# One row of w4 by loads of 125 and 3 partitions of its own

## The chip, the core and the metric

The kernel runs on one core of a Trainium2 chip. The metric is the device time of one execution, in microseconds (us). The core has five engines with instruction streams of their own: PE (matrix products, with weight loads shown as PEld), DVE (vector work), ACT (activation functions), POOL and SP. Data come from the chip's main memory by 16 DMA engines. SP issues almost all loads here; a load is cut into packets that the 16 DMA engines carry, and each DMA engine works through its packets of SP's queue in the order of issue.

## What is computed

The reference decodes one token (x has shape 1 x 1 x 1024). It normalises x, sends it through an attention block over a cache of 65,536 keys and through a small MLP block, and adds x and both results:

```python
def reference(A_x, A_k_cache, A_v_cache, A_wq, A_wo, B_x, B_w1, B_w2, B_w3, B_w4):
    ...
    xn = _layernorm(x, axis=-1)
    return x + _A_ref(xn, A_k_cache, A_v_cache, A_wq, A_wo) + _B_ref(xn, B_w1, B_w2, B_w3, B_w4)
```

`_A_ref` makes 32 query heads of 128 with wq, scores them against 4 groups of cached keys, takes the softmax, sums the cached values and multiplies by wo. `_B_ref` is two gelu layers with w1 and w2, then `gelu(layernorm(x1) @ w3) @ w4`, with 1024 inputs, 3584 hidden values and 1024 outputs, so w4 is 3584 x 1024. With one token, the shifted rows between w1 and w2 are all zero, and nearly all the time is reading: 170 MB of caches and weights, in bf16.

## The kernel before

Every large operand passes through one of three slots (`big`, `SLOTS = 3`) of 128 partitions by 64 KB. The list `items` gives the order of loading and of work: wq, K(0,0), V(0,0), w3, w12 (w1 and w2 in one slot), then K and V of the four groups and two halves of the keys, with w4 put in just ahead of the last V, and at the end wo in three slots (pieces of 20, 8, and 3 + 1 rows of 1024, `WO_PIECES`). So the end of the list is K(3,1), w4, V(3,1), wo 0, wo 1, wo 2.

`ensure` keeps the loads two items ahead of the work (`LOOKAHEAD = 2`): before item i is worked on, item i + 2 is issued. `issue` (L96 and below) takes a slot, builds the list `loads` of source and place, and issues each on SP (L118 and L119). SP waits there until the slot's former content has been used, and the next load waits behind it in SP's stream. A K load is 128 packets of 64 KB, 8 on each DMA engine; w4 was one load (L104): partition m takes the rows 28m to 28m + 27 of w4, 28 rows of 1024 bf16 values, 57,344 bytes.

The work on an item: `compute_K` transposes the keys on DVE (L337), multiplies them by the queries on PE (L340), finds the maximum (L344), and makes the exponentials (L357) and their transposes (L359). `compute_V` multiplies these by the values (L393). `compute_w4` makes 28 x 4 small products (`row_acc`, L161), each with one row of 1024 of a partition, which add to psB; `compute_wo` does the same with wo, and after its last piece copies psB (L435) and stores the result (L436). Two small loads of x are issued by ACT at the start; the one at L130 brings x as 4 rows of 512 bytes to the partitions 0, 32, 64 and 96.

Of the kernel before, what the change touches and what calls it, by code (L numbers as in the profile page):

```python
# [22 lines left out]
def kernel(  # L23
# [14 lines left out]
    nc = tc.nc  # L38
    P = 128
# [9 lines left out]
    FC = F // P  # L49
    NOUT = A_wo.shape[1]  # L50
# [23 lines left out]
    wq_v = A_wq.rearrange("(p c) n -> p (c n)", c=DC)  # L74
    w3_v = B_w3.rearrange("(p c) f -> p (c f)", c=DC)
    w4_v = B_w4.rearrange("(m c) n -> m (c n)", c=FC)
    wo_v = A_wo.rearrange("(m c) n -> m c n", c=OC)
    w1_v = B_w1.rearrange("(p c) n -> p (c n)", c=DC)
    w2_v = B_w2.rearrange("(m c) n -> m (c n)", c=DC)
# [16 lines left out]
    def issue(item):  # L96
        kind = item[0]
        t = big.tile([P, KEYS], BF16, name="slot")
        if kind == "wq":
            loads = [(0, wq_v)]  # L100
        elif kind == "w3":
            loads = [(0, w3_v)]
        elif kind == "w4":
            loads = [(0, w4_v)]  # L104
        elif kind == "w12":
            loads = [(0, w1_v), (KEYS // 2, w2_v)]
        elif kind == "wo":
            pieces = [item[1]] if item[1] < 2 else list(range(2, len(WO_PIECES)))
            loads = []
            for q in pieces:  # L110
                c0 = wo_start[q]
                at = (c0 - wo_start[pieces[0]]) * NOUT
                loads.append((at, wo_v[:, c0:c0 + WO_PIECES[q], :].rearrange("p c n -> p (c n)")))
        else:
            cache = A_k_cache if kind == "K" else A_v_cache
            _, g, r = item
            loads = [(0, cache[0, g, r * KEYS:(r + 1) * KEYS, :].rearrange("(p k) d -> p (k d)", p=P))]
        for at, src in loads:  # L118
            nc.sync.dma_start(out=t[:, at:at + src.shape[-1]], in_=src)  # L119
        st[item] = t  # L120

    x_bf = const.tile([P, DC], BF16, name="x_bf")
# [11 lines left out]
    def ensure(upto):  # L134
        while n_issued[0] <= min(upto, len(items) - 1):
            issue(items[n_issued[0]])
            n_issued[0] += 1
# [30 lines left out]
    def layernorm(src, tag):  # L168
# [50 lines left out]
                          in_=sel8[:].unsqueeze(2).to_broadcast([P, 8, 4]))  # L219

    iv = ident_bf[:].rearrange("p (b i r) -> p b r i", b=2, r=2)
    for b in range(2):
        for par in range(2):
            nc.vector.tensor_copy(out=psel[:, 2 * b + par, :].rearrange("p (a i) -> p a i", a=4),
                                  in_=iv[:, b, par, :].unsqueeze(1).to_broadcast([P, 4, 32]))
# [4 lines left out]
                          in_=lead.unsqueeze(2).to_broadcast([P, 4, 16]))  # L230
    gsel = const.tile([P, P], BF16, name="gsel")
    nc.vector.tensor_copy(out=gsel[:].rearrange("p (j m) -> p j m", j=2),
                          in_=lead[:, 0:2].unsqueeze(2).to_broadcast([P, 2, 64]))
# [239 lines left out]
```

## Time and profile before

Three runs took 402.79, 402.89 and 403.63 us. The profile is of another execution:

| what | value |
|---|---|
| median of three runs | 402.89 us |
| the profiled execution's own time | 402.66 us |
| its span, from the first instruction to the last | 400.9 us |
| granted PE clock, mean | 0.796 |
| busy: PE, DVE, ACT, POOL | 204.0, 209.0, 27.3, 5.9 us |
| read by DMA | 169.87 MB, 424 GB/s over the span |
| w4's load: issue, and landing of its last share | 323.72, 358.62 us |
| w4's products on PE (L161 with hT) | from 363.01 us on |

The span divided into 40 slices shows the same picture from the first to the last but one (the DMA row is the mean busy share of the 16 DMA engines in tenths, below it GB/s):

```profile
DMA  9999999999999999999999999999999999999994
GB/s 406 425 425 419 419 420 452 401 489 419 425 433 419 419 484 427 419 432 438 420 419 471 432 420 438 438 420 438 451 419 425 433 445 436 419 455 419 414 416 174
```

PE and DVE are each busy for about half of the span and idle in between; the DMA engines are not. The loads that matter for the change are these (KB of one, and the time from issue to landing in us; the first line is w3 and w4 together, the last is the fourth piece of wo, 2,048 bytes for each of 128 partitions):

```profile
slot<-in_B_w_dram SPq DMA_DIRECT2D x2, 7168.0 KB, 37.7
...
slot<-in_A_wo_dram SPq DMA_DIRECT2D x1, 5120.0 KB, 27.0
...
slot<-in_A_wo_dram SPq DMA_DIRECT2D x1, 2048.0 KB, 26.3
slot<-in_A_wo_dram SPq DMA_DIRECT2D x1, 768.0 KB, 13.5
slot<-in_A_wo_dram SPq DMA_DIRECT2D x1, 256.0 KB
```

### The profile page before, as it was taken

The numbers are of one execution on the slowest core, as the hardware profiler recorded it, in microseconds if no ns is written. First come the engines' busy times: TensorE is split into PE (matmuls) and PEld (weight loads), VectorE is DVE, ScalarE is ACT, GpSimd is POOL, SyncE is SP. The second block draws the span as 40 slices with busy tenths as digits, with TensorE's granted clock in tenths as the row PEclk, the third lists the DMA queues.
The fourth block names the chain that finished last, engine by engine and source line by source line (L and its number), as shares of the span: only waits on it lengthen the run. The fifth ranks groups of instructions, "written<-read, shape, count | busy, mean of one in ns | idle before, by whom it ended". The sixth has DMA issues, their size and how long they took to land.

```text
span 400.9 us, 3366 instructions
## 1 busy us (share of the span) xinstructions
PE 204.0 (51%) x1489; PEld 85.4 (21%) x1489; DVE 209.0 (52%) x190; ACT 27.3 (7%) x33; POOL 5.9 (1%) x27
## 2 busy tenths in 40 slices
PE   0016393660079148741965295529453935496235
PEld 0003131220023013310322042204121412143113
DVE  0022992230196559634954894279358841885120
ACT  0002002110000300020002000100200020002000
POOL 1010000000000000000000000000000000000000
PEclk9999698695569587967895689679975976599588
DMA  9999999999999999999999999999999999999994
GB/s 406 425 425 419 419 420 452 401 489 419 425 433 419 419 484 427 419 432 438 420 419 471 432 420 438 438 420 438 451 419 425 433 445 436 419 455 419 414 416 174
DMA packets 3773, 170.07 MB, mean 424 GB/s; under 512 B 552, under 2 KB 560, under 8 KB 816
## 3 DMA queue, kind: packets, MB, share of 16 engines
q1 hardware_dynamic: 3608, 169.87, 98.1%
q8 instruction: 11, 0.18, 0.2%
q10 hardware_dynamic: 152, 0.00, 0.0%
q14 instruction: 2, 0.02, 0.0%
HBM read 169.87 MB, written 0.00 MB: 424 GB/s over the span
## 4 chain that ended last, share of the span: by engine, by line
DMA 48%; PE 26%; DVE 20%; ACT 4%; issue 1%; ACTq 0%; SPq 0%; POOL 0%; DVEq 0%
DMA slot<-in_A_k_cache_dram 28%; PE sc L340 14%; DVE slot L337 12%; DMA slot<-in_A_v_cache_dram 10%; PE oacc L393 8%; DMA work<-in_A_x_dram 7%; DMA slot<-in_A_wo_dram 3%; DVE work L359 3%; DVE mx L344 3%; ACT work L357 3%; PE rows L242 1%; ACT L357 1%; PE pm_mx L346 0%; DVE m L348 0%; DVE og L408 0%
## 5 line engine op out<-in xcount | busy, mean ns | idle before, releaser
L340 PE MATMUL sc<-slot,qst 128*128 128x512 bf16 x512 | 129.8, 415 | 75.6 <-DVE slot L337 75.6
L337 DVE STREAM_TRANSPOSE slot<-slot 128x4096 f32<-128x4096 f32 x32 | 139.4, 4413 | 49.4 <-DMA slot<-in_A_k_cache_dram 49.3
L340 PEld LDWEIGHTS <-qst 128*128 128x128 bf16 x512 | 52.1, 103 | 152.1 <-DVE slot L337 55.9
L393 PE MATMUL oacc<-slot,work 128*32 128x512 bf16 x512 | 43.3, 513 | 45.3 <-DVE work L359 35.7
L344 DVE TENSOR_REDUCE mx<-sc 128x1 f32<-128x2048 f32 x8 | 18.3, 2292 | 30.2 <-PE sc L340 30.2
L393 PEld LDWEIGHTS <-work 128*32 128x32 bf16 x512 | 16.3, 124 | 69.2 <-DVE work L359 36.3
L357 ACT ACTIVATE work<-sc,nball 128x2048 bf16<-128x2048 f32 x8 | 15.7, 1967 | 193.5 <-DVE nball L355 193.5
L359 DVE STREAM_TRANSPOSE work<-work 128x2048 bf16<-128x2048 bf16 x8 | 18.5, 2311 | 19.1 <-ACT work L357 19.1
L408 DVE SCALAR_TENSOR_TENSOR og<-oacc,wm,og 128x128 f32<-128x128 f32 x16 | 5.6, 351 | 22.2 <-PE oacc L393 21.8
L172 PE MATMUL pm_ln<-ln_rowsum_a,work 128*128 128x1 f32 x2 | 0.6, 362 | 27.7 <-POOL work L147 27.7
L166 DVE CAST xT<-x_bf 128x8 f32<-128x8 bf16 x1 | 0.2, 172 | 22.0 <-DMA x_bf<-in_A_x_dram 22.0
L346 PE MATMUL pm_mx<-ident_f,mx 128*1 128x128 f32 x8 | 2.3, 283 | 18.1 <-DVE mx L344 18.1
L242 PE MATMUL rows<-slot,xpad 128*32 128x512 bf16 (+1 forms) x144 | 9.6, 397 | 0.9 <-DMA slot<-in_B_w_dram 0.9
L161 PE MATMUL psB<-slot,oT 128*1 128x256 bf16 x128 | 6.3, 362 | 6.3 <-DMA slot<-in_A_wo_dram 6.1
L357 ACT ACT_TABLE_LOAD x2 | 2.6, 1283 | 73.5 <-DVE nball L355 73.5
L287 DVE TENSOR_TENSOR work<-pm_h,mask 128x448 f32<-128x448 f32 x1 | 0.6, 625 | 11.4 <-PE pm_h L284 11.4
L172 PEld LDWEIGHTS pm_ln<-ln_rowsum_a,work 128*128 128x128 f32 x2 | 0.5, 310 | 27.6 <-POOL work L147 27.6
L435 DVE CAST work<-psB 97x256 bf16<-97x256 f32 x1 | 0.4, 425 | 11.4 <-PE psB L161 11.4
L161 PEld LDWEIGHTS <-oT 128*1 128x1 bf16 x128 | 3.9, 108 | 8.8 <-issue 5.6
L242 PEld LDWEIGHTS <-xpad 128*32 128x32 bf16 x144 | 4.4, 103 | 5.7 <-DMA slot<-in_B_w_dram 1.8
L346 PEld LDWEIGHTS pm_mx<-ident_f,mx 128*1 128x1 f32 x8 | 0.6, 79 | 21.9 <-DVE mx L344 21.9
L412 PE MATMUL pm_e<-og,sel8x 128*32 128x129 f32 x8 | 1.6, 282 | 6.6 <-DVE og L408 6.6
(102 smaller groups left out, 65.4 us busy)
## 6 DMA issues: line engine op xcount, KB each, us to landing
slot<-in_B_w_dram SPq DMA_DIRECT2D x2, 7168.0 KB, 37.7
slot<-in_A_wo_dram SPq DMA_DIRECT2D x1, 5120.0 KB, 27.0
slot<-in_B_w_dram SPq DMA_DIRECT2D x2, 2048.0 KB, 23.1
slot<-in_A_wo_dram SPq DMA_DIRECT2D x1, 2048.0 KB, 26.3
slot<-in_A_wo_dram SPq DMA_DIRECT2D x1, 768.0 KB, 13.5
slot<-in_A_wo_dram SPq DMA_DIRECT2D x1, 256.0 KB
slot<-in_A_k_cache_dram SPq DMA_DIRECT2D x8, 41.7
slot<-in_A_v_cache_dram SPq DMA_DIRECT2D x8, 38.6
```

Source lines behind the costliest of these rows:

```text
L161: nc.tensor.matmul(psB[32 * j:32 * j + 1, 0:NQ], lhsT=lhsT, rhs=w_row[:, NQ * j:NQ * (j + 1)], start=False, stop=False, tile_position=(0, ...
L172: nc.tensor.matmul(pm[:, 0:1], lhsT=ones_f, rhs=rowsum[:], start=True, stop=True)
L242: nc.tensor.matmul(acc[32 * j:32 * j + 32, bk, 0:width], lhsT=xp[:, c, :], rhs=wt[:, c, ch * width:(ch + 1) * width], start=(c == 0), stop ...
L337: nc.vector.transpose(out=kf[:, cg, :], in_=kf[:, cg, :])
L340: nc.tensor.matmul(sc[:, hf, :], lhsT=qst[g % 2][:, bp, 24 - 8 * cg:24 - 8 * cg + P], rhs=kr[:, cg, hf, :, bp // 2, :, bp % 2], start=(cg ...
L344: nc.vector.reduce_max(out=mx[:], in_=sc[:].rearrange("p h n -> p (h n)"), axis=AX.X)
L346: nc.tensor.transpose(pm[0:1, 0:P], mx[:, 0:1], ident_f[:])
L357: nc.scalar.activation(out=pT, in_=sc[:], func=ACTF.Exp, bias=nball[:, r:r + 1], scale=SCALE, accum_out=lall[:, r:r + 1])
L359: nc.vector.transpose(out=pT, in_=pT)
L393: nc.tensor.matmul(oacc[32 * u:32 * (u + 1), :], lhsT=pT[:, hf, 32 * t:32 * (t + 1)], rhs=vt[:, :, hf, t, :], start=(hf == 0 and t < 4), s ...
L408: nc.vector.scalar_tensor_tensor(out=og[:, 0:P], in0=oacc[:, P * cg:P * (cg + 1)], scalar=wm[:, 1, cg:cg + 1], in1=og[:, 0:P], op0=ALU.mul ...
L412: nc.tensor.matmul(pe[rows, 0:P + 1], lhsT=sel8x[:], rhs=og[:], start=True, stop=True, tile_position=(0, 32 * g))
```

## The change

w4's single load becomes three, issued one after the other on SP. The first brings rows 0 to 26 of every partition's 28 (55,296 bytes for each of 128 partitions). The second brings row 27 (2,048 bytes) of partitions 0 to 124, the third that of partitions 125 to 127. The bytes, their places in the slot and the work on them stay the same.

```diff
@@ -74,6 +74,7 @@
     w4_v = B_w4.rearrange("(m c) n -> m (c n)", c=FC)
+    W4_REST = P // 5 * 5
@@ -101,7 +102,7 @@
         elif kind == "w4":
-            loads = [(0, w4_v)]
+            loads = [(0, w4_v[:, 0:(FC - 1) * NOUT])]
@@ -117,6 +118,10 @@
         for at, src in loads:
             nc.sync.dma_start(out=t[:, at:at + src.shape[-1]], in_=src)
+        if kind == "w4":
+            last = slice((FC - 1) * NOUT, FC * NOUT)
+            nc.sync.dma_start(out=t[0:W4_REST, last], in_=w4_v[0:W4_REST, last])
+            nc.sync.dma_start(out=t[W4_REST:P, last], in_=w4_v[W4_REST:P, last])
         st[item] = t
```

## The prediction

> **What bounds the kernel now.** I read the table of DMA queues first.
>
> ```profile
> q1 hardware_dynamic: 3608, 169.87, 98.1%
> q8 instruction: 11, 0.18, 0.2%
> q10 hardware_dynamic: 152, 0.00, 0.0%
> q14 instruction: 2, 0.02, 0.0%
> ```
>
> SP's loads (q1) fill the 16 DMA engines for 98% of the span, so only what makes these engines finish later or earlier counts. Next, the end of the chain of waits (start, duration, what):
>
> ```profile
> 337.88 40.06 DMA slot<-in_A_v_cache_dram
> 377.95 0.14 issue
> 378.08 5.03 PE oacc L393 x60
> 383.11 0.02 issue
> 383.13 0.33 SPq L119
> 383.46 0.05 issue
> 383.51 13.81 DMA slot<-in_A_wo_dram
> 397.32 0.04 issue
> 397.36 0.31 PE psB L161 x4
> 397.67 0.02 issue
> 397.69 0.42 DVE work L435
> ```
>
> The last piece of wo is issued at 383.51 and lands at 397.32, not because 1 MB is slow, but because it stands behind what is queued before it. Four matmuls, a copy and the store follow: a fixed tail to 400.9. The end is thus the landing on the latest engine. How unequal the engines are, the table of stretches shows (stretch, length, busy time of PE, PEld, DVE, ACT, POOL, PE clock, DMA share, GB/s):
>
> ```profile
> 392.00:394.00 2.00, 2.00 (x44) 1.30 (x40) 0.00 (x0) 0.00 (x0) 0.00 (x0) 0.50 1.00 418
> 394.00:395.00 1.00, 0.65 (x16) 0.27 (x12) 0.00 (x0) 0.00 (x0) 0.00 (x0) 0.73 0.62 256
> 395.00:396.00 1.00, 0.95 (x32) 0.66 (x27) 0.00 (x0) 0.00 (x0) 0.00 (x0) 1.00 0.46 182
> 396.00:397.00 1.00, 0.29 (x12) 0.26 (x12) 0.00 (x0) 0.00 (x0) 0.00 (x0) 1.00 0.16 64
> 397.00:398.00 1.00, 0.49 (x12) 0.10 (x4) 0.31 (x1) 0.00 (x0) 0.00 (x0) 1.00 0.00 0
> ```
>
> The DMA share falls from 1.00 to 0.62, 0.46 and 0.16: the engines run out in steps, over 3 us. The trace's packet records (queue, start, length, bytes) say who is late: on a full queue a packet starts within a few ns of the end of the one before it, so each engine's sequence can be followed, 200 data packets each. Seven engines end their last packet at 394.1 to 394.6, six at 395.7 to 396.1, three at 396.8 to 396.97. What sets them apart are the q8 packets: 16 KB in 0.88 to 0.97 us, and the packet behind one takes 0.47 to 0.55 us more, some 1.4 us in all. Three engines had two, five had one; the sixth of the middle group had two q14 packets at 0.83 us.
>
> **The change, removed.** Each of the 16 engines has 8 packets of w4's 7,168 KB load. They shrink from 57,344 to 55,296 bytes. A 65,536-byte packet takes 2,418 ns, so 2,048 bytes are 75.6 ns, eight times that 0.60 us less on every engine.
>
> **Added: packets.** The same 256 KB come back as 128 packets of 2,048 bytes. The nearest row is the last load of wo, with just such packets: 84 ns each, one every 80 ns.
>
> **Where they go.** A load of 128 rows puts 8 packets and one completion on each of 16 engines: q1 has 404 completion packets of 4 bytes, 25 loads by 16 plus 4 for the store of 4 rows. The 4-row load of L130 has four packets of 512 bytes, one on each of four engines. So rows are shared out evenly. 125 rows go evenly over 5 engines (25 each) or over 1; 3 rows over 3. I take 5 and 3: 25 x 80 ns = 2.00 us on five engines, 0.08 us more on three. Net +1.40 to +1.48 us on the five, -0.60 us on the other eleven. [...] Bounds: spread over 16 engines nearly nothing is added (8 x 80 ns - 0.60 = +0.04 us); on one engine 125 x 80 ns - 0.60 = +9.4 us.
>
> **Which engines.** If a small load takes the same first engines each time, four of the five are those with L130's packets: two that end at 394.2 and 394.3, two at 395.8 and 396.0. The fifth is one of the other twelve. With +1.4 us on the later of these, 396.0 becomes 397.4; the three latest fall from 396.97 to 396.4. The end moves by +0.45 us.
>
> **What one engine's packets meet.** The disputed price is the 2 KB packet. All 64 KB packets take 2,418 ns (27.1 GB/s), and wo's 6 KB packets 234 ns whether 16 engines run or three. So the limit isn't a total: it is private to each engine, or to the eight partitions that it writes. In every load of before each engine has 8 rows, so the trace can't tell these apart. In the new load an engine has 25 rows, and at most 8 of them can be its usual partitions; the others are those of engines that are by then running the next load, V, at their full rate. If the limit sits with the partitions, two streams share 27.1 GB/s and a 2 KB packet takes 160 ns (estimate: twice 80). Lower bound 80 ns (wo's row). Upper bound from the only row where an engine carries something beside its stream: the 16 KB instruction packet, 1.43 us in place of 0.61, a factor 2.35, 188 ns. I take 160 ns, nearer to the second, since that packet too isn't one of an engine's own eight rows. Between 17 and all 25 at 160 ns, the rest at 80: 3.4 to 4.0 us; less 0.60, plus 0.08 to 0.16 for the 3-row load: +2.8 to +3.5 us on the loaded engines. The engine ending at 396.0 then ends at 398.8 to 399.5, a fifth engine of the latest three at 399.8 to 400.5. The engines written over lose at most what they gained (8 x 75 ns). Against 396.97: +1.8 to +3.5 us, I take +2.5. [...]
>
> **Other costs, all covered.** SP's two more issues: 0.33 us each. SP issues w4 at 323.72 and next at 337.88, when V's slot comes free: 13.5 us of idle time hide them, and V stands no earlier in the queue.
>
> ```profile
> 323.72 0.33 SPq L119 DMA_DIRECT2D slot<-in_B_w_dram  x1
> 337.88 0.33 SPq L119 DMA_DIRECT2D slot<-in_A_v_cache_dram  x1
> 363.11 20.82 SPq L119 DMA_DIRECT2D slot<-in_A_wo_dram  x4
> ```
>
> w4's matmuls wait for all three loads. They start at 363.01, behind K's; w4 lands at 358.62 now, at worst at 358.62 - 0.60 + 4.16 = 362.2. Were that cover gone, PE still idles 9.55 us before V's landing. V's own landing (377.95) moves with the late engine, so do L393 and the last wo issue (383.5 to some 386); the quickest engines need those packets at 391, after 8 packets of wo's second piece (611 ns each) from 386.2 on. So the queue doesn't run dry. SP's wait for wo's second piece now names three loads of w4 instead of one; they have landed long before 368.6.
>
> **Sum.** The profiled execution took 402.66 us (span 400.9), 0.23 under the median of 402.89. 402.66 + 2.5 = 405.2, and with a little for the median 405.3.
>
> **Rivals.**
> 1. *The engine is the limit, not the partitions*: +0.45 us, 403.1 to 403.3. For it: the 512-byte packets of L130, which go to partitions 0, 32, 64 and 96, took 25 to 27 ns, no more than 9 ns plus 18.9 for their bytes. Against: they are tiny, and a write that waits behind needn't show in them. Chance 0.20.
> 2. *The same, but the fifth engine is one of the three latest* (3 of 12): 396.97 + 1.40, so 404.1 to 404.3. Chance 0.07.
> 3. *The load evens the engines out* (the other side): if the five are all among the seven that have 2.4 us to spare, 394.5 + 1.48 stays below 396.4 and the end comes 0.60 us earlier, 402.1 to 402.3. It decides if no loaded engine ends after 394.9 now and a 2 KB packet stays near 80 ns; two of L130's four engines speak against it. That is also the most the change can give, since no engine loses more than 16 KB. Chance 0.06.
> 4. *Nothing is concentrated*, 125 rows spread over 16 engines: +0.04 us, 402.7 to 402.9. Against it the even shares above. Chance 0.06.
> 5. *One engine has all 125*: +8 us or more, some 411. Chance 0.03.
>
> **How the numbers follow.** Sharing has 0.58, with its own range 403.9 to 406.6 (part of the rows shared, to the factor 2.35: 25 x 188 ns - 0.60 + 0.19 = +4.3 on 396.0, +3.3). Its time is the prediction. The range goes down to 402.8 to take in rivals 1 and 2 and half of 4. Under 0.2% (0.8 us, about what a measurement of this kernel can tell from no change) stand rivals 1, 3 and 4, together 0.32, of which I give 0.03 to a gain beyond 0.8 us from something not seen; slower 0.68 from sharing, 2 and 5.
>
> **What would show it.** Packet records: 125 packets of 2 KB on five engines, with lengths near 84 ns (rival 1) or 160 (sharing), and the V packets of other engines longer at that time. Stretches: the DMA share in the last microseconds should end in one or two engines (0.06 to 0.13) for 2 us longer. The chain should still end in V, L393 and wo's DMA, shifted as a whole. The prediction is wrong if wo's last piece lands within 0.8 us of 397.3, or if another kind of wait shows up in the chain.

## The result, and the profile after

The changed kernel took 404.35 us in the median of seven runs (404.28 to 404.52), against 402.89 (402.79 to 403.63): +1.46 us, a ratio of 1.0034 with the interval [1.0023, 1.0046]. It is slower, by a third of a percent, which is clear of the noise. The profiled execution took 404.31 us, with a span of 402.5.

The end of the chain of waits has the shape of before (start, duration, what), and is later as a whole:

```profile
336.75 42.99 DMA slot<-in_A_v_cache_dram
379.74 0.14 issue
379.87 4.92 PE oacc L398 x60
384.79 0.02 issue
384.80 0.33 SPq L120
385.13 0.05 issue
385.18 13.90 DMA slot<-in_A_wo_dram
399.08 0.04 issue
399.13 0.31 PE psB L166 x4
```

V lands at 379.74 (377.95 before), wo's last piece at 399.08 (397.32): +1.8 us at both places. So the time was lost before V landed, and nothing after it gave any back. The table of stretches of the changed kernel shows the last microseconds (stretch, length, busy time of PE, PEld, DVE, ACT, POOL, PE clock, DMA share, GB/s):

```profile
394.00:395.00 1.00, 1.00 (x25) 0.63 (x21) 0.00 (x0) 0.00 (x0) 0.00 (x0) 0.50 0.89 371
395.00:396.00 1.00, 1.00 (x24) 0.68 (x17) 0.00 (x0) 0.00 (x0) 0.00 (x0) 0.50 0.83 346
396.00:397.00 1.00, 0.56 (x20) 0.28 (x15) 0.00 (x0) 0.00 (x0) 0.00 (x0) 0.95 0.64 254
397.00:398.00 1.00, 0.73 (x28) 0.46 (x18) 0.00 (x0) 0.00 (x0) 0.00 (x0) 1.00 0.23 92
398.00:399.00 1.00, 0.49 (x12) 0.28 (x12) 0.00 (x0) 0.00 (x0) 0.00 (x0) 1.00 0.04 16
```

From 398 on the share is 0.04: of 16 engines one is left, for 0.7 us. The queue's line of the changed kernel says how many engines the new loads use:

```profile
q1 hardware_dynamic: 3744, 169.87, 98.1%
```

There are 136 packets more than the 3608 of before: 128 of data, and 8 completions, which is 5 + 3 engines.

And the place of the loss is seen when the stretch in which w4 ends and V begins is set side by side (same columns). Before:

```profile
354.00:362.00 8.00, 7.42 (x35) 3.19 (x34) 5.39 (x2) 0.00 (x0) 0.00 (x0) 1.00 1.00 433
```

After:

```profile
354.00:362.00 8.00, 8.00 (x38) 3.54 (x37) 5.36 (x2) 0.00 (x0) 0.00 (x0) 1.00 1.05 374
```

The DMA engines are as busy as before (share 1.00 and 1.05), but move 374 GB/s instead of 433. A busy share alone would have hidden this. A row counts a packet's whole length and bytes in the stretch in which it starts, so the share can pass 1.00; the two are best divided: 433 GB/s at a full share before, 356 after. The packet records tell the rest. Four of the five loaded engines have their 25 small packets from 354.7 to 357.5, the fifth from 357.35 to 359.89. The packets take 84 to 140 ns, 107 in the mean. In just that time every engine, loaded or not, is slow: V's first 64 KB packets take up to 3,436 ns in place of 2,418. Each engine without small packets loses 1.37 to 1.54 us, 26 to 30% of the 5.2 us that the loads last. The ends of the engines' last packets, us:

| engines | before | after |
|---|---|---|
| three latest (two instruction packets each) | 396.8 to 397.0 | 397.9 to 398.0 |
| five of the middle group | 395.7 to 396.1 | 396.6 to 397.0 |
| the one with the two q14 packets, loaded | 395.96 | 398.74 |
| three early ones, not loaded | 394.1 to 394.6 | 394.9 to 395.5 |
| four early ones, loaded | 394.1 to 394.6 | 396.6 to 397.0 |

The engine with the q14 packets (called the table engine from here on; only a name) sets the end. Its account: -0.60 for the shorter w4 packets, +2.54 for 25 packets from 357.35 to 359.89, +0.85 lost on its last w4 and first V packet: +2.79, and 395.96 became 398.74. Against the 396.97 of the latest engine of before this is +1.77.

### The profile page after: what moved, and what is told of

Its sections match the earlier page's. It is cut to its first block, busy times and chain, and to the rows that moved or that the text cites. A ratio compares the mean times of both kernels' runs of the same rounds, so it can differ in the third digit from the quotient of the medians.

```text
span 402.5 us, 3369 instructions
## 1 busy us (share of the span) xinstructions
PE 206.7 (51%) x1489; PEld 86.5 (22%) x1489; DVE 208.9 (52%) x190; ACT 27.3 (7%) x33; POOL 6.0 (1%) x27
## 3 DMA queue, kind: packets, MB, share of 16 engines
q1 hardware_dynamic: 3744, 169.87, 98.1%
## 4 chain that ended last, share of the span: by engine, by line
DMA 49%; DVE 30%; PE 16%; ACT 4%; issue 1%; ACTq 0%; SPq 0%; POOL 0%; DVEq 0%
DMA slot<-in_A_k_cache_dram 28%; DVE slot L342 22%; DMA slot<-in_A_v_cache_dram 11%; PE oacc L398 8%; DMA work<-in_A_x_dram 6%; PE sc L345 5%; DMA slot<-in_A_wo_dram 3%; DVE work L364 3%; DVE mx L349 3%; ACT work L362 3%; PE rows L247 1%; ACT L362 1%; DVE og L413 0%; DVE m L353 0%; PE pm_mx L351 0%
## 5 line engine op out<-in xcount | busy, mean ns | idle before, releaser
L398 PE MATMUL oacc<-slot,work 128*32 128x512 bf16 x512 | 44.4, 523 | 47.5 <-DVE work L364 35.7
L247 PE MATMUL rows<-slot,xpad 128*32 128x512 bf16 (+1 forms) x144 | 10.5, 426 | 0.1
```

Of the source, the lines that this page charges most:

```text
L247: nc.tensor.matmul(acc[32 * j:32 * j + 32, bk, 0:width], lhsT=xp[:, c, :], rhs=wt[:, c, ch * width:(ch + 1) * width], start=(c == 0), stop ...
L398: nc.tensor.matmul(oacc[32 * u:32 * (u + 1), :], lhsT=pT[:, hf, 32 * t:32 * (t + 1)], rhs=vt[:, :, hf, t, :], start=(hf == 0 and t < 4), s ...
```

## The experiments

Three theories stood against each other. A: a write into partitions that another engine is just writing slows the engines. (Below, such writes are called crossing. That each engine writes the same eight partitions in every load of 128 rows was my assumption; no packet record names a partition.) B: only the number of packets on an engine counts. C (and later D): something else about the new loads, their small pieces far apart in memory, or their running on fewer than 16 engines, slows everything. Each kernel was timed beside the kernel before.

**One load of 128 partitions** (in place of those of 125 and 3):

```diff
-            nc.sync.dma_start(out=t[0:W4_REST, last], in_=w4_v[0:W4_REST, last])
-            nc.sync.dma_start(out=t[W4_REST:P, last], in_=w4_v[W4_REST:P, last])
+            nc.sync.dma_start(out=t[0:128, last], in_=w4_v[0:128, last])
```

> The last row of w4 comes by one load of 128 partitions, the same 2,048-byte pieces with the same 56 KB between them, 8 on each engine. Theory A (a write into partitions that another engine is writing slows both): nothing is crossed, 8 x 80 ns - 0.60 us = +0.04 us, within 0.2 us of before. Theory B (only the number of packets on one engine counts): the same +0.04 us. Theory C (small pieces read 56 KB apart slow every engine): all engines lose again the 1.4 us that they lost in the changed kernel, +0.8 to +1.4 us.

Measured 402.90 us, ratio 0.9998 [0.9988, 1.0007]. All 128 small packets took 84 ns and V's first packets 2,418. The same reads, in the same pieces, cost nothing: C falls.

**Loads of 96 and 32 partitions**, and **of 64 and 64** (the same edit with 64; both against the changed kernel):

```diff
-            nc.sync.dma_start(out=t[0:W4_REST, last], in_=w4_v[0:W4_REST, last])
-            nc.sync.dma_start(out=t[W4_REST:P, last], in_=w4_v[W4_REST:P, last])
+            nc.sync.dma_start(out=t[0:96, last], in_=w4_v[0:96, last])
+            nc.sync.dma_start(out=t[96:128, last], in_=w4_v[96:128, last])
```

> The last row comes by loads of 96 and 32 partitions: 6 and 2 rows on each of 16 engines, as many packets per engine as with 128 partitions, but rows of partitions that another engine writes in the loads around it. A: the packets take more than 84 ns and all engines lose time, +0.3 to +1.4 us. B: +0.05 us. C: as for the load of 128 partitions.

> Loads of 64 and 64 partitions, 4 and 4 rows on each of 16 engines. A: in each load 16 engines write the partitions of some 8, so packets take about 160 ns, 8 x 160 - 600 ns = +0.7 us. B: +0.05 us. C: as for the load of 128 partitions.

Measured 403.99 us, ratio 1.0026 [1.0017, 1.0036], and 403.94 us, 1.0026 [1.0016, 1.0036]. The queue's line has 160 packets more than before with 96 and 32, so 2 x 16 completions: all engines take part, none is loaded more than another, and still 1.0 us is lost. Most engines lose 0.7 to 0.9 us in w4's last and V's first packets, so B alone can't be the whole. With 64 and 64 the small packets took 99 ns in the mean, not the 160 that A had forecast; the loss showed in V's packets behind them.

**Loads of 127 and 1 partitions** (the same edit with 127):

> Loads of 127 and 1 partitions. If rows are shared out evenly, one engine gets all 127 (no other number up to 16 divides 127): B: 128 x 80 ns - 0.60 = +9.6 us on an engine that ended up to 1 us before the last, so +8.6 to +9.6 us. A: its packets take 100 to 130 ns as in the changed kernel, +11 to +15 us, and the other engines lose a quarter of their speed for as long. If rows are spread unevenly over 16 engines: under +0.5 us.

Measured 410.52 us, ratio 1.0189 [1.0173, 1.0204], +7.5 us: one engine has all 127, 354.8 to 365.9, but an early one (its last packet ends at 404.93; 394.2 - 0.60 + 127 x 0.088 = 404.8), where I had reckoned with a late one. This run is confounded, as SP's own stream shows (start, duration; the L124 line is the load of one partition):

```profile
323.52 0.32 SPq L123 DMA_DIRECT2D slot<-in_B_w_dram  x1
323.88 32.90 SPq L124 DMA_DIRECT2D slot<-in_B_w_dram  x1
356.88 0.36 SPq L120 DMA_DIRECT2D slot<-in_A_v_cache_dram  x1
```

The issue of the next small load took 32.90 us instead of some 0.3: SP stood until some 2 us after the one engine had begun with its small packets. V was issued at 356.88, 19 us later than before, and most engines had run dry from 355 on (DMA share 0.66 from 354 to 358, 1.09 before). So the time can't be held against either account. The packets still show the slowing, and by a single engine. On each of the other fifteen engines V's second 64 KB packet, begun at 361.1 to 362.0 while the one engine wrote its rows, took 3,114 to 3,273 ns, and from 367.1 on, when that engine was done, such packets took 2,418 again.

**Own partitions or others'.** The next kernels leave w4 whole, as before, and add loads that nothing reads, with everything alike but the partitions that they write:

```diff
+        if kind == "w4":
+            for j in range(4):
+                nc.sync.dma_start(out=t[j + 0:j + 0 + 29:4, FC * NOUT:FC * NOUT + 2048],
+                                  in_=w4_v[j:j + 29:4, 0:2048])
```

The variant above is meant to write the engines' own partitions. In place of j + 0 the others have j + 64 (meant as other engines' partitions), j + 4 (the neighbours') and j + 32 (the upper half of the own). Which engine writes which partition was assumed, and the names below follow that; the runs test it only by whether V's packets lengthen. The two variants with five rows, with j + 0 and j + 64, have 17 and 4096 in place of 29 and 2048.

> w4 comes whole, as before; behind it four loads of 8 rows by 4,096 bytes bring copies of w4 values to the unused end of the slot, which nothing reads: rows to partitions j, j+4 ... j+28. They run on 8 engines, 4 packets each, 0.63 us. If these partitions are the engines' own eight of a 128-row load, theory A (a write into partitions that another engine is writing slows the engines) has V's packets at 2,418 ns as before, and the end moves by 0 to +0.63 us, by whether one of the latest engines is among the eight. Theory D (any load on fewer than 16 engines slows all) has V's packets at 2.9 to 3.4 us and +0.4 to +1.3 us. [...]

> The same four loads with the same sources, but to partitions 64 + j, 68 + j ... 92 + j, which other engines write. A: V's packets lengthen on all engines that are written over, half the bytes of the loads of 96 and 32 partitions, so about half of their loss of 0.85 us: +0.3 to +0.5 us more than with the engines' own partitions. D: the same time as with the own partitions.

Measured: own partitions 402.81 us, ratio 0.9997 [0.9987, 1.0006]; partitions 64 and up 404.25 us, 1.0031 [1.0019, 1.0043]. The stretch from 354 to 362 again, with own partitions:

```profile
354.00:362.00 8.00, 8.00 (x39) 3.51 (x37) 5.46 (x2) 0.00 (x0) 0.00 (x0) 1.00 1.04 449
```

and with those of other engines:

```profile
354.00:362.00 8.00, 7.78 (x37) 3.35 (x36) 5.55 (x2) 0.00 (x0) 0.00 (x0) 1.00 1.05 399
```

The same sources, bytes and number of packets (3672 on q1 in both, 32 of data and 4 x 8 completions more than before), nearly the same busy share, and 399 GB/s instead of 449. V's packets took 2,418 ns in the first and up to 3,358 in the second. D falls, A stands. But the loss, 1.44 us over the own partitions, was some three times what I expected (+0.3 to +0.5 us), and its spread doesn't fit A as I had it: all 16 engines lost 0.7 to 1.1 us, also the eight loading ones, into whose own partitions, as assumed, nobody else wrote.

**Five engines, own partitions and others':**

> Four loads of 5 rows by 8,192 bytes behind w4, to partitions j, j+4 ... j+16, again to the unused end of the slot: 4 packets, 1.21 us, on each of five engines, and to their own partitions. The term of concentration alone. A: V's packets stay at 2,418 ns, the latest of the five engines moves from 396.0 to 397.2 (span time of before), +0.2 us; +1.2 us if one of the three latest is among the five. D: another +0.5 to +1.4 us for all.

> The same with partitions 64 + j ... 80 + j: five engines, the same bytes, other engines' partitions. A: the loss of all engines comes back, 160 KB against the changed kernel's 250 KB that cost each engine 1.4 us, so some +0.5 to +0.9 us over the loads to the own partitions. D: no difference from them.

Measured: own 402.71 us, ratio 0.9995 [0.9986, 1.0004]; others' 405.22 us, 1.0055 [1.0038, 1.0072]. In the run with own partitions the five loaded engines are in plain sight: four of the early ones, and the table engine, which ends at 397.18, as expected. So concentration by itself costs next to nothing here, with 1.21 us of packets on each of the five. With the crossing, the 8 KB packets, 309 ns alone, take 606 to 656 ns where they meet a running stream, twice as long, as if two streams shared what one had. The engines without such packets lose 1.37 to 1.51 us (one 2.41). The 2.51 us over the own partitions are far more than the +0.5 to +0.9 expected: the table engine needs 2.02 us for its four packets instead of 1.21, loses 1.57 us on its large ones, and ends last, at 399.62.

**Neighbours, and the upper half of the own partitions:**

> The four loads of 8 rows by 4,096 bytes once more, now to partitions 4 + j, 8 + j ... 32 + j: each engine writes the partitions of its neighbour, the last of the eight those of the first, all within the lower 64 partitions. If any partition of another engine costs, as with partitions 64 to 95: +1.0 to +1.4 us, V's packets at 2.9 to 3.3 us. If only the upper half is far for the first eight engines: like the own partitions, within 0.3 us of before.

> The same to partitions 32 + j, 36 + j ... 60 + j. If these are the other half of the eight partitions that each of the first eight engines has in a 128-row load, nothing lengthens, within 0.3 us of before; if an engine has eight partitions in a row (8i to 8i + 7), these are other engines' and it costs +1.0 to +1.4 us.

Measured: the neighbours' partitions 403.55 us, ratio 1.0024 [1.0014, 1.0034]; partitions 32 to 63 403.04 us, 1.0003 [0.9994, 1.0013]. With the neighbours' partitions, +0.73 us lies between the two accounts, and its ten runs spread wide, from 403.32 to 404.81; V's packets took up to 3,311 ns. With 32 to 63 all V packets took 2,418, as with 0 to 31. So, by A, both halves of the lower 64 partitions count as these engines' own. And with the neighbours' (partitions 4 to 35, within those 64) the eight engines that by this neither load nor are written over lost 0.60 to 0.73 us each, although the crossing packets of seven of the eight loading engines took 159 ns, as to their own partitions.

**Dose, and four engines:**

> Twice the dose: the last two rows (4,096 bytes) of w4 by loads of 125 and 3 partitions, the first 26 by 128. The account by now: the end is set by the latest of the five loaded engines (396.0 in the span of before, against 396.97 for the latest of all), and that engine pays for its 25 packets and, with all others, for the slowing while the crossing lasts. Additive: -1.21 (two rows less) + 25 x 0.155 (a 4,096-byte packet takes 159 ns, one follows 4 ns before its end) + 2 x 1.4 - 1.0 = +4.5 us. If the slowing does not grow with the bytes: -1.21 + 3.9 + 1.4 - 1.0 = +3.1 us. If only packets counted: -1.21 + 3.9 - 1.0 = +1.7 us.

> Loads of 124 and 4 partitions: shared out evenly over 4 engines, 31 + 1 rows on each. The table engine (two q14 packets) is then still loaded if it is one of the first four: -0.60 + 32 x 0.08 + 1.4 to 1.8 - 1.0 = +2.4 to +2.8 us. If it is the fifth, the loaded four end at 394.3 + 3.4 to 3.8 = 397.7 to 398.1 and the unloaded latest at 396.97 + 0.8 to 1.2, so +0.8 to +1.2 us, less than the changed kernel in spite of more packets per engine.

Two rows: 408.26 us, ratio 1.0136 [1.0121, 1.0151], +5.4 us, more than the additive account (+4.5). The 4 KB packets took 253 ns in the mean, where 155 were reckoned, and engines without them lost 3.1 us and more, against 1.4 with one row: the slowing grows at least with the bytes. 124 and 4: 405.55 us, 1.0066 [1.0049, 1.0083], +2.67 us, within the first of the two accounts: the table engine is one of the four loaded ones, and has 32 packets instead of 25. The sum is made up otherwise, though: 3.55 us of packets instead of 2.6, and 1.02 us of slowing instead of 1.4 to 1.8. The profile's end, 124 and 4:

```profile
398.00:399.00 1.00, 0.95 (x32) 0.66 (x29) 0.00 (x0) 0.00 (x0) 0.00 (x0) 1.00 0.17 66
399.00:400.00 1.00, 0.27 (x12) 0.25 (x12) 0.00 (x0) 0.00 (x0) 0.00 (x0) 1.00 0.06 23
```

A single engine (0.06 of 16) works until 399.96.

Side by side, an engine without small packets loses the more, the longer the crossing lasts: 0.94 to 1.11 us in 3.3 us (eight engines, partitions 64 and up), 1.37 to 1.54 in 5.2 (the changed kernel), about 2.0 in 6.2 (124 and 4), 3.1 to 3.8 in 9.4 (two rows).

## Why the prediction was right, and where it wasn't

It gave slower, 405.3 us, and 404.35 was measured, inside the range that begins at 402.8 and inside that of sharing, 403.9 to 406.6. Point by point:

- *What bounds the kernel* was right: the landing on the latest DMA engine, with a fixed tail. The chain moved as a whole.
- *Five and three engines* was right, by the 8 completions; the even shares alone had left five or one open. The runs with 96, 124 and 127 rows agree with even shares, with 32, 8 and 2 completions more than before. Right too were the 0.60 us saved and the covers: two issues on SP of 0.37 and 0.26 us, with V's issue at 336.75 still waiting for its slot alone.
- *Which engines* was wrong in part: I had two of L130's four engines ending early and two late. The five are four early ones and the table engine. My sequences had lost their identity where two engines' packets end within a few ns of each other. The step still gave the right late engine, 395.96, which was in part luck.
- *The loaded engine's price*, +2.8 to +3.5 us, came out at +2.78, but made up differently. The 2 KB packet was mis-sized: 107 ns in the mean and 140 at most, not 160, so 25 of them took 2.54 us, not 3.4 to 4.0. The rest, 0.85 us, it lost on its 64 KB and 55 KB packets, a term that the prediction doesn't have. That the total came out at the edge of its span is luck: one term too large and one left out nearly cancel.
- *"The engines written over lose at most what they gained"* is the step that failed. All engines lost 0.6 to 1.5 us by the slowing, and those without small packets 1.37 to 1.54, where the step allowed 0.60 at most. These gained only 0.60 back, so they all ended later than before, by 0.7 to 1.2 us.
- *The end*: I took +2.5 us from the middle of +1.8 to +3.5; the span's last packet moved by +1.77, the lower end, since the packets cost less than supposed and the fifth engine wasn't a late one. The median moved by 1.46, and the time of the two profiled executions by 1.65 (402.66 to 404.31).
- *The rivals*: none of the five took the place of the forecast, though the sharing that it rests on fits only the packets that meet (8 KB in 606 to 656 ns in place of 309). Rival 1 (the engine is the limit) is excluded by the pair with as many engines and other partitions (402.81 and 404.25 us). Rival 3 (a gain) failed because the slowing reaches all engines, and because the table engine, which ended at 396.0, is one of the five.
- *The signs* came in part: 125 packets on five engines, but at 107 ns, between the 84 and the 160 named; V's packets longer, but on all engines; and one engine left at the end, for 0.7 us instead of 2.

Taken apart, the loss is mostly the crossing: loads with no engine favoured cost +1.0 us by crossing alone, and five engines favoured without crossing cost nothing, with 1.21 us of packets each. With both, the table engine has 2.54 us of packets on top of the slowing, and ends 0.7 us behind the latest of the others.

What stays open: why engines that, as assumed, neither write across nor are written over lose too (0.60 to 0.73 us with the neighbours' partitions). The runs show that it happens with writes into other engines' partitions, ends with them, and grows with the time that they last, but not what these engines share with the others. A lighter load on the partitions of the late engines, which might use the early ones' spare 2.5 us without crossing, was not tried.

## What to carry to other kernels

On this kernel's full DMA queue (98.1%), bringing the last row by one load of 128 partitions cost nothing (ratio 0.9998), and every split of it by partitions cost time, +1.0 us with 96 and 32 or 64 and 64, +1.46 with 125 and 3, +2.67 with 124 and 4: keep to loads of 128 partitions, and don't split a load by partitions to even out engines. Look at GB/s beside the DMA share, and compare stretches: a share of 1.05 with 374 GB/s, against 1.00 with 433, was a slowdown that the share hid. The end of this kernel was set by its latest engine (396.97 before, 398.74 after), so follow single engines before pricing an edit.

## What the hardware showed that I had not expected

- Writes meant for other engines' partitions slowed all 16 engines: 128 KB to partitions 64 to 95 cost each 0.7 to 1.1 us, and 128 KB to partitions 4 to 35 cost at least 0.60 us each even the eight whose partitions, as assumed, they don't touch. One writing engine was enough: V's 64 KB packets took 3,114 to 3,273 ns on the other fifteen, and 2,418 when it was done.
- The load of 127 partitions, whose rows one engine carried behind a full queue, held the next issue on SP for 32.90 us.
- Extra packets to the engines' own partitions cost nothing measurable: 160 KB more by four early engines and the table engine, ratio 0.9995 [0.9986, 1.0004].
- A 16 KB instruction packet set its DMA engine back by some 1.4 us (0.88 to 0.97 us for itself, 0.47 to 0.55 us more for the packet behind it), and three engines with two of them set the end of the kernel before, at 396.8 to 396.97.
